# Pooled attention feeding a fast-matrix mixture of experts: ScalarE seeds the second product's bank, GpSimd keeps one sum, attention is placed a chunk ahead

## The chip, the core and the metric

The kernel runs on one core of a Trainium2 chip. Five engines work from queues of their own, each in order: TensorE (PE, with its weight loads PEld), VectorE (DVE), ScalarE (ACT), GpSimd (POOL) and SyncE (SP). They wait for each other, and for transfers, by semaphores. The metric is device time in microseconds; lower is better.

## The reference

Attention with pooled keys and values feeds a dense mixture of four experts. There are 8 batches, 8 heads, 576 tokens and a head size of 64.

```python
k_p = k.reshape(B, H, Sp, 8, D).mean(axis=3)          # 72 pooled keys
v_p = v.reshape(B, H, Sp, 8, D).mean(axis=3)
attn = softmax(q @ k_p^T / sqrt(D))
x = (attn @ v_p)  as  [B * S, H * D] = [4608, 512]
p = domain_probs / domain_probs.sum(-1)
for e in range(4):                                    # w1: 512 x 1024, w2: 1024 x 512
    out += p[:, e:e + 1] * (relu(x @ w1[e]) @ w2[e])
```

The inputs are float32; the kernel multiplies in bfloat16 and sums in float32.

## The kernel before, in words

**Chunks and tasks.** The 4608 tokens are cut into nine chunks of 512: for each batch its first 512 tokens, and a ninth chunk of the eight remainders of 64. A task is one chunk with one expert: the up product (x by w1, then ReLU, giving H) and the down product (H by w2, scaled by the token's probability and added to `acc`). Chunk 0 is done in four early stages with plain products, except for its first down product. The other 32 tasks run in one loop.

**Seven products.** In the loop each product of two matrices cut in quarters is made with seven quarter products in place of eight, from sums and differences of quarters. Of the activations these are `x_sums` (up) and `hidden_sums` (down); of the weights, `first_weight_sums` and `weight_sums`. All of them are VectorE instructions of line 186. The partial results grow in two banks of PSUM. `up_product` (L483) does this for two units of the hidden dimension, with two banks each (`units`). In step 0 ScalarE copies product 1 from bank 0 to SBUF (`partial`, L512) because it is part of several results. Step 1 makes product 2 in bank 1, and VectorE adds the copy, applies ReLU and writes a quarter of H, all in one custom instruction (`relu_sum`, L481). Steps 2 and 3 grow in bank 0 and are copied to `partial` too. Steps 4 and 6 end in `relu_sum`, step 5 in ScalarE's ReLU (L520). `down` (L550) uses the two banks `chains`; which comes first alternates from task to task. After each step two blocks of 128 tokens are added to `acc`. That is done by VectorE (`add`, L635), by ScalarE for the first write of expert 0 (L633), or, for steps in `POOLED = (1, 4, 6)` of experts 1 to 3, by ScalarE scaling into `addend` (L576) and GpSimd adding that (L578).

**Slots.** The loop counts slots `g`, seven to a task. In each slot TensorE makes step i of unit 0, step i - 1 of unit 1 (four matmuls each) and step i - 1 of the down product of the task before (eight matmuls), all with 256 columns. The order in which the program emits its instructions is by hand, and it is each engine's order. Hidden sums stand at the end of slots 0 to 3 of a task, after the reads of that slot. Pieces of attention for the next chunk are attached to slots of the 28-slot chunk (`pieces_at`).

**Attention of a batch.** GpSimd issues the loads. From batch 2 on keys and values come in four parts of two pooled rows, where parts 1 to 3 add onto the buffer during the transfer (`load_part`, L118; part 0 is L120); each therefore waits for the one before. VectorE adds the last two rows (`fold_keys`, L220; `fold_values`, L261). SP issues transposing transfers for q (`queries`, L272), keys (`keys`, L226) and, for each quarter of 128 tokens, for the context (`turn`, L339). TensorE makes `scores` (L299) and `context` (L325), ScalarE the exponential (L303), VectorE the division (L313, L314). `x_sums` needs all four turns of the batch. The remainders of two batches at a time go the same way (`rem_queries`, `rem_scores`, `rem_context`, `rem_turn`). Batch 1 is prepared in the early stages (`pieces_first`), from whole loads.

**Stores.** When expert 3 has finished a quarter of `acc`, SP stores it (L643); the next chunk's expert 0 writes that quarter again.

Of the kernel before, what the change touches and what calls it, by code (L numbers as in the profile page):

```python
# [17 lines left out]
def kernel(  # L18
# [10 lines left out]
    nc = tc.nc  # L29
# [45 lines left out]
    acc = const.tile([P, NR, DM], F32, name="acc")  # L75
    x_rem = const.tile([P, NPAIR, NT], BF16, name="x_rem")
# [174 lines left out]
    def idle(n):  # L251

        w_ps = work_bank()
        for _ in range(n):
            nc.tensor.matmul(w_ps, lhsT=zeros[:, 0:P], rhs=zeros)  # L255

# [226 lines left out]
    def up_product(c, e, unit, step):  # L483
# [5 lines left out]
            (1, False, b21, a12),  # L489
# [21 lines left out]
        if step == 0 or step == 3:  # L511
            nc.scalar.copy(out=part[:, 0], in_=ps)  # L512
        elif step == 2:
            nc.scalar.copy(out=part[:, 1], in_=ps)  # L514
        elif step == 1:
            relu_sum(quarter(0, 0), ps, part[:, 0])
        elif step == 4:
            relu_sum(quarter(1, 1), ps, part[:, 0])
        elif step == 5:
            nc.scalar.activation(out=quarter(0, 1), in_=ps, func=ACT.Relu)  # L520
        else:
            relu_sum(quarter(1, 0), ps, part[:, 1])
# [27 lines left out]
    def down(c, e, step, flip=0, pooled=()):  # L550
# [5 lines left out]
            lambda: (1, False, a12, w[:, HI, 0:HD], 0, 0, False),  # L556
# [16 lines left out]
        if step in pooled and e > 0:  # L573
            for j in range(BLOCKS):
                prob = p_all[:, c * NR + row * BLOCKS + j, e:e + 1]
                nc.scalar.activation(out=addend[:, j], in_=ps[:, j], func=ACT.Copy, scale=prob)  # L576
            dst = acc[:, row * BLOCKS:(row + 1) * BLOCKS, cols]
            nc.gpsimd.tensor_add(out=dst, in0=dst, in1=addend[:])  # L578
        else:
            for j in range(BLOCKS):  # L580
                add(ps[:, j], c, e, row * BLOCKS + j, cols, first)
# [80 lines left out]

    def pieces_first():
# [25 lines left out]
        put(3, 1, lambda: load_part(2, 1))  # L689
        put(3, 3, lambda: load_q(2))  # L690
# [4 lines left out]
    def pieces_at(b):  # L695

        at = {}

        def put(slot, piece):
            at.setdefault(slot, []).append(piece)  # L700

        if b < B:
            late = b == BUSY
            put(4 if late else 0, lambda: queries(b))
            put(5 if late else 0, lambda: fold_keys(b, every))
            put(6 if late else 1, lambda: keys(b, every))
            put(7 if late else 5, lambda: fold_values(b, every))
            for pair, slot in enumerate((9, 11, 12, 13) if late else (6, 8, 12, 13)):
                put(slot, lambda pair=pair: scores(b, pair))
            for r in range(NR):  # L710
                put((14, 16, 19, 21)[r], lambda r=r: context(b, r))
                put((15, 17, 20, 22)[r], lambda r=r: turn(b, r))
            put(26, lambda: x_sums(b))
            if late:
                put(1, lambda: load_part(b, 3))
                put(2, lambda: load_q_rem(b))
            if b + 1 < B:
                put(8 if late else 6, lambda: load_part(b + 1, 0))
                put(9 if late else 8, lambda: (load_q(b + 1), load_q_rem(b + 1)))
                put(12, lambda: load_part(b + 1, 1))  # L720
                put(17, lambda: load_part(b + 1, 2))
                put(22, lambda: load_part(b + 1, 3))
        if b % 2 == 0 and b <= B:
            i = b // 2 - 1
            put(0, lambda: rem_queries(i))
            put(4, lambda: rem_scores(i))
            put(7, lambda: rem_context(i))
            put(8, lambda: rem_turn(i))
        if b == B:
            put(12, lambda: x_sums(B))  # L730
        return at

    ENG = mybir.EngineType
    with tc.manual_schedule(
# [13 lines left out]
        load_whole(1, v, "vraw")  # L748
        load_w2(1)
        load_w1(3)  # L750
# [6 lines left out]
        first_pieces = pieces_first()  # L757

        for s, (above, below) in enumerate(
                [((0, 1), None), ((0, 2), (0, 0)), ((0, 3), (0, 1)), (None, (0, 2))]):  # L760
            if s == 1:
                hidden_sums(*below, 0)
                hidden_sums(*below, 1)
            for i in range(FCH):
                if above:
                    up(*above, (i,))
                if below and s != 1 and i % 2:
                    down_plain(*below, i // 2)
# [9 lines left out]
        units[0] = [psum_last.tile([P, NT], F32, name=f"unit0{i}") for i in range(2)]  # L778

        N = len(order)
        below_of = [(0, 3)] + order
        sums = {}
        for at, pieces in (((2, 3, 4, 5), first_weight_sums(2)), ((9, 10, 12, 13), weight_sums(2)),
                           ((16, 17, 18, 19), first_weight_sums(3))):
            sums.update(zip(at, pieces, strict=True))
        POOLED = (1, 4, 6)
        for g in range(7 * N + 1):
            t, i = divmod(g, 7)  # L790
            if t < N:
# [4 lines left out]
            if g >= 1:  # L796
                down(*below_of[t2], i2, t2 % 2, POOLED)
            if i < 4 and t < N:
                hidden_sums(*below_of[t], i)
            if t < N:  # L800
                c = order[t][0]
                at = pieces_at(c + 1)
                for piece in at.get(g - 7 * E * (c - 1), ()):
                    piece()
            if g in sums:
                sums[g]()
# [31 lines left out]
```

## Time and profile before

| | us |
|---|---|
| median of 4 runs | 515.4 (513.71 to 516.87) |
| the profiled execution | 516.33 |
| its span, first to last instruction | 514.6 |
| TensorE busy | 496.9 (97%) |
| VectorE busy | 405.6 (79%) |
| ScalarE busy | 291.9 (57%) |
| GpSimd busy | 181.9 (35%) |

The costliest groups beside TensorE are the 192 ReLU sums (131.3 us, 684 ns each), the 246 additions to `acc` of 256 columns (107.2, 477 ns), GpSimd's 72 additions (95.9, 1331 ns), ScalarE's 128 copies of line 512 (74.9, 585 ns) and its 144 scalings of line 576 (60.5, 471 ns).

A line of the timeline reads: start, length, engine, line, operation, tile written and tiles read, shape, count, and in brackets the idle time of the engine just before with what ended it. A line of the waits reads: who waited, for whom, the total in us, how often, the longest. "DMA kpT<-kp" is the transfer that writes the tile kpT from kp. A group's mean length of a matmul (273 ns for 256 columns) includes its way through the array; from start to start it is 109 ns. Idle time of an engine other than the bound costs nothing by itself.

### The profile page before, as it was taken

How to read it: one execution, taken by the hardware profiler on the slowest of the kernel's cores; microseconds unless marked ns; L12 is line 12 of the kernel's file. 1: busy time of each engine (PE TensorE's matmuls, PEld its weight loads, DVE VectorE, ACT ScalarE, POOL GpSimd, SP SyncE). 2: the span in 40 equal slices, each digit the busy share in tenths (PEclk: the TensorE clock that was granted, in tenths of full speed). 3: DMA queues.
4: the chain of work that ended last, by engine and by line, in shares of the span. 5: the costliest groups of instructions: out<-in, count | busy, mean ns of one | idle time of the engine just before them, and what ended most of it. 6: DMA issues, size and time to landing. Idle time of an engine off the chain costs nothing.

```text
span 514.6 us, 11532 instructions
## 1 busy us (share of the span) xinstructions
PE 496.9 (97%) x4578; PEld 407.6 (79%) x4578; DVE 405.6 (79%) x776; ACT 291.9 (57%) x557; POOL 181.9 (35%) x160
## 2 busy tenths in 40 slices
PE   9999897899899999999999999999999999999996
PEld 4656345678777988888878888888888888888885
DVE  3556387969997898788978896889788878877873
ACT  2675513575457656755576567655765565556550
POOL 6331053424445353535363536253102311222131
PEclk9999899989999999999999999999999999999998
DMA  9999999895819491948294849775102020003003
GB/s 190 210 206 208 186 89 88 147 87 56 75 35 153 41 100 36 150 44 95 43 143 38 94 56 114 73 88 55 64 19 35 20 75 2 0 22 83 1 1 83
DMA packets 106790, 42.51 MB, mean 83 GB/s; under 512 B 79840, under 2 KB 105184, under 8 KB 106736
## 3 DMA queue, kind: packets, MB, share of 16 engines
q0 software_dynamic: 59728, 22.43, 41.2%
q1 hardware_dynamic: 46432, 18.82, 19.1%
q8 instruction: 36, 0.59, 0.5%
q10 hardware_dynamic: 576, 0.52, 0.3%
q14 instruction: 18, 0.15, 0.1%
HBM read 45.69 MB, written 9.44 MB: 107 GB/s over the span
## 4 chain that ended last, share of the span: by engine, by line
PE 79%; DMA 10%; DVE 7%; issue 2%; ACT 1%; POOL 0%; DVEq 0%
PE unit L500 34%; PE o_ps L567 33%; DMA w_bf<-in_moe_w_dram 5%; DMA xT<-x_tok 3%; PE unit L255 2%; PE unit L448 2%; PE att L299 1%; PE unit L619 1%; PE o_ps L590 1%; DVE H L481 1%; DVE acc L635 1%; PE att L325 1%; DVE H L186 1%; DMA kpT<-kp 1%; DVE wu_bf L186 1%
## 5 line engine op out<-in xcount | busy, mean ns | idle before, releaser
L578 POOL TENSOR_TENSOR acc<-acc,addend 128x512 f32<-128x512 f32 x72 | 95.9, 1331 | 256.5 <-ACT addend L576 132.3
L481 DVE CUSTOM_DVE_ANT_0 H<-unit,partial 128x512 bf16<-128x512 f32 x192 | 131.3, 684 | 29.0 <-PE unit L500 26.3
L635 DVE SCALAR_TENSOR_TENSOR acc<-o_ps,p_all,acc 128x256 f32<-128x256 f32 (+1 forms) x254 | 113.2, 485 | 46.1 <-PE o_ps L567 34.2
L567 PEld LDWEIGHTS <-H 128*128 128x128 bf16 x1320 | 129.0, 98 | 17.1 <-DVE H L186 1.2
L500 PEld LDWEIGHTS <-w_bf 128*128 128x128 bf16 x1024 | 96.9, 98 | 17.4 <-issue 6.2
L512 ACT COPY partial<-unit 128x512 f32<-128x512 f32 x128 | 74.9, 585 | 57.2 <-PE unit L500 56.3
L567 PE MATMUL o_ps<-w_bf,H 128*128 128x256 bf16 x792 | 102.6, 273 | 0.0
L500 PE MATMUL unit<-xT,w_bf 128*128 128x256 bf16 x672 | 96.4, 273 | 1.4 <-DVE H L481 0.7
L576 ACT ACTIVATE addend<-o_ps,p_all 128x256 f32<-128x256 f32 x144 | 60.5, 471 | 53.5 <-PE o_ps L567 53.5
L500 PEld LDWEIGHTS <-wu_bf 128*128 128x128 bf16 x768 | 74.6, 98 | 12.7 <-DVE xs L186 2.4
L500 PE MATMUL unit<-xs,wu_bf 128*128 128x256 bf16 x512 | 77.6, 274 | 2.1 <-DVE xs L186 2.1
L567 PE MATMUL o_ps<-wt_bf,H 128*128 128x256 bf16 x528 | 68.5, 273 | 0.6 <-DVE H L186 0.6
L567 PEld LDWEIGHTS <-S 128*128 128x128 bf16 x528 | 51.8, 99 | 9.7 <-DVE S L186 2.9
L514 ACT COPY partial<-unit 128x512 f32<-128x512 f32 x64 | 38.0, 594 | 19.7 <-PE unit L500 18.9
L520 ACT ACTIVATE H<-unit 128x512 bf16<-128x512 f32 x64 | 38.2, 596 | 19.0 <-PE unit L500 18.9
L118 POOL DMA_DIRECT2D kraw<-in_k_dram x18 | 25.1, 1395 | 37.9 <-DMA kraw<-in_k_dram 37.9
L500 PE MATMUL unit<-xs,w_bf 128*128 128x256 bf16 x256 | 38.5, 273 | 0.0
L303 ACT ACTIVATE expT<-att 72x1024 bf16<-72x1024 f32 x28 | 28.5, 1018 | 15.8 <-PE att L299 15.8
L633 ACT ACTIVATE acc<-o_ps,p_all 128x256 f32<-128x256 f32 x72 | 30.2, 471 | 12.5 <-PE o_ps L567 10.0
L567 PE MATMUL o_ps<-wt_bf,S 128*128 128x256 bf16 x264 | 35.1, 277 | 2.1 <-DVE S L186 2.1
L118 POOL DMA_DIRECT2D vraw<-in_v_dram x18 | 33.9, 1885 | 3.6 <-DMA vraw<-in_v_dram 3.6
L567 PE MATMUL o_ps<-w_bf,S 128*128 128x256 bf16 x264 | 34.2, 273 | 0.0
(106 smaller groups left out, 486.8 us busy)
## 6 DMA issues: line engine op xcount, KB each, us to landing
out_dram<-acc SPq DMA_DIRECT2D x32, 256.0 KB, 2.5
w_bf<-in_moe_w_dram POOLq DMA_DIRECT2D x7, 1024.0 KB, 22.3
q_sb<-in_q_dram POOLq DMA_DIRECT2D x7, 512.0 KB, 9.5
kraw<-in_k_dram POOLq DMA_DIRECT2D x24, 144.0 KB, 6.2
vraw<-in_v_dram POOLq DMA_DIRECT2D x24, 144.0 KB, 8.0
acc<-in_q_dram SPq DMA_DIRECT2D x2, 512.0 KB, 4.7
w_bf<-in_moe_w_dram POOLq DMA_DIRECT2D x2, 512.0 KB, 11.6
wt_bf<-in_k_dram POOLq DMA_DIRECT2D x2, 288.0 KB, 7.6
```

The lines of the kernel that those rows point to most:

```text
L118: nc.gpsimd.dma_start(out=raw[:], in_=rows, accum_op=ALU.add)
L303: nc.scalar.activation(out=expT[:, 2 * pair:2 * pair + 2].rearrange("j h a b t -> j b (h a) t"), in_=sc_ps[0:SP].rearrange("j b h (a t) -> ...
L481: nc.vector._custom_dve(TENSOR_ADD_SAT, out=dst, in0=ps, in1=part, s0=LARGEST, s1=0.0)
L500: nc.tensor.matmul(ps[:, n * HN:(n + 1) * HN], lhsT=lhs[:, kc, f:f + P], rhs=rhs[:, kc, :], start=(not grows and n == 0 and kc == 0), stop ...
L512: nc.scalar.copy(out=part[:, 0], in_=ps)
L514: nc.scalar.copy(out=part[:, 1], in_=ps)
L520: nc.scalar.activation(out=quarter(0, 1), in_=ps, func=ACT.Relu)
L567: nc.tensor.matmul(ps[:, j], lhsT=lhs[:, i, j * P:(j + 1) * P], rhs=rhs[:, i, :], start=(not grows and i == 0 and j == 0), stop=(i == HF - 1),
L576: nc.scalar.activation(out=addend[:, j], in_=ps[:, j], func=ACT.Copy, scale=prob)
L578: nc.gpsimd.tensor_add(out=dst, in0=dst, in1=addend[:])
L633: nc.scalar.activation(out=dst, in_=o_ps, func=ACT.Copy, scale=prob)
L635: nc.vector.scalar_tensor_tensor(out=dst, in0=o_ps, scalar=prob, in1=dst, op0=ALU.mult, op1=ALU.add,)
```

## The change

- `up_product`: ScalarE copies product 1 from bank 0 into bank 1 of PSUM. Product 2 grows on top of it, and ScalarE applies ReLU to the result. Two ReLU sums per unit are left to VectorE, which add the results of steps 2 and 3.
- `down`: in the same way product 1 is copied from one bank into the other, where product 2 grows. The additions to `acc` after step 0 fall away; step 1 adds the sum. `POOLED` is `(4,)`: GpSimd does one sum per task, steps 1 and 6 go to VectorE.
- `open_bank` makes one matmul in each of two banks before they are first grown on.
- Hidden sums 0, 2 and 3 stand at the start of their slots, hidden sum 1 after unit 1's product.
- Plain products of chunk 0's experts 1 and 2 stand at other places; the last one stands in slot 0 of the loop.
- w1 of expert 3 is loaded ahead of w2 of expert 1.
- `gate`: a small GpSimd copy reads one element of each of the four turns of batch 1. It stands ahead of part 1 of batch 2 in GpSimd's queue.
- `pieces_later` gives each batch's attention its slots. For batches 4 to 7 q, keys and values are prepared in the last four slots of the chunk before, the turns are in slots 9, 10, 12 and 14, and the loads of the next batch in slots 0, 1, 4, 7 (keys and values) and 17 (q). Batches 2 and 3 have slots of their own. The fold of batch 2's keys is still in slot 5, its first scores move from 9 to 11. Weight sums move by some slots.

```diff
+    def open_bank(ps):
+        nc.tensor.matmul(ps, lhsT=ident[:], rhs=w2_bf[:, 0, 0, :], skip_group_check=True)
...
-            (1, False, b21, a12),
+            (1, True, b21, a12),
...
-        if step == 0 or step == 3:
-            nc.scalar.copy(out=part[:, 0], in_=ps)
-        elif step == 2:
-            nc.scalar.copy(out=part[:, 1], in_=ps)
+        if step == 0:
+            nc.scalar.copy(out=units[unit][1][:], in_=ps)
+        elif step == 2 or step == 3:
+            nc.scalar.copy(out=part[:, step - 2], in_=ps)
         elif step == 1:
-            relu_sum(quarter(0, 0), ps, part[:, 0])
+            nc.scalar.activation(out=quarter(0, 0), in_=ps, func=ACT.Relu)
         elif step == 4:
-            relu_sum(quarter(1, 1), ps, part[:, 0])
+            relu_sum(quarter(1, 1), ps, part[:, 1])
...
-            relu_sum(quarter(1, 0), ps, part[:, 1])
+            relu_sum(quarter(1, 0), ps, part[:, 0])
...
-            lambda: (1, False, a12, w[:, HI, 0:HD], 0, 0, False),
+            lambda: (1, True, a12, w[:, HI, 0:HD], 0, 0, True),
...
-        if step in pooled and e > 0:
+        if step == 0:
+            nc.scalar.copy(out=chains[(1 + flip) % 2][:], in_=chains[flip][:])
+        elif step in pooled and e > 0:
...
+    def gate():
+        nc.gpsimd.tensor_copy(out=gate_at[:], in_=state[("xT", 1)][0:1, 0, 0:NT:P])
...
-        put(3, 1, lambda: load_part(2, 1))
-        put(3, 3, lambda: load_q(2))
+        put(3, 1, gate, lambda: load_part(2, 1))
+        put(3, 2, lambda: load_q(2))
...
-    def pieces_at(b):
+    def pieces_later():
...
+        for b in range(2, B + 1):
+            start = 7 * E * (b - 2)
+            if b < B:
+                q_at, k_at, scores_at, contexts_at, loads_at = {
+                    2: (4, 5, (11, 12, 13, 17), (18, 19, 20, 22), (8, 10, 9, 12, 15)),
+                    3: (0, 1, (6, 11, 12, 13), (16, 18, 19, 20), (4, 6, 5, 8, 11)),
+                }.get(b, (-4, -4, (3, 4, 5, 6), (8, 9, 11, 13), (0, 17, 1, 4, 7)))
+                put(start + q_at, lambda b=b: queries(b))
+                put(start + k_at, lambda b=b: fold_keys(b, every))
+                put(start + k_at + 1, lambda b=b: keys(b, every), lambda b=b: fold_values(b, every))
...
+            if b == 2:
+                put(1, lambda: load_part(2, 3))
+                put(2, lambda: load_q_rem(2))
...
+            put(start + 26, lambda b=b: x_sums(b))
...
+        load_w1(3)
         load_w2(1)
-        load_w1(3)
...
+        plain_at = {(2, 2): 0, (2, 4): 1, (2, 6): 2, (2, 7): 3}
+        plain_at.update({(3, 2 * r + 1): r for r in range(NR - 1)})
...
+                open_bank(chains[1][:])
...
+        open_bank(units[0][1][:])
...
-        POOLED = (1, 4, 6)
+        POOLED = (4,)
         for g in range(7 * N + 1):
             t, i = divmod(g, 7)
+            if i in (0, 2, 3) and t < N:
+                hidden_sums(*below_of[t], i)
             if t < N:
                 up_product(*order[t], 0, i)
             t2, i2 = divmod(g - 1, 7)
             if 0 <= t2 < N:
                 up_product(*order[t2], 1, i2)
-            if g >= 1:
+            if i == 1 and t < N:
+                hidden_sums(*below_of[t], i)
+            if g == 0:
+                down_plain(0, 2, NR - 1)
+            else:
                 down(*below_of[t2], i2, t2 % 2, POOLED)
-            if i < 4 and t < N:
-                hidden_sums(*below_of[t], i)
```

## The prediction

> **What bounds the kernel now.** I read the page first, then TensorE's waits, then the busy time by stretches, then the timelines around each wait.
>
> ```profile
> span 514.6 us, 11532 instructions
> PE 496.9 (97%) x4578; PEld 407.6 (79%) x4578; DVE 405.6 (79%) x776; ACT 291.9 (57%) x557; POOL 181.9 (35%) x160
> ```
>
> TensorE is the bound; every other engine has room. Only its pauses can be won back, and any new pause in the loop is lost whole. Its waits, over the whole run:
>
> ```profile
> PE att L299 <- DMA kpT<-kp: 2.1, 1, 2.1
> PE o_ps L567 <- DVE S L186: 2.1, 3, 1.0
> PE unit L500 <- DVE xs L186: 2.1, 1, 2.1
> PE unit L448 <- DMA w_bf<-in_moe_w_dram: 2.0, 1, 2.0
> ...
> PE unit L500 <- DVE H L481: 0.7, 2, 0.4
> PE o_ps L567 <- DVE H L186: 0.6, 2, 0.3
> ```
>
> The stretches (us, PE busy, PEld, DVE, ACT, POOL, granted clock, DMA share, GB/s) say where:
>
> ```profile
> 53.70:60.00 6.30, 6.28 (x26) 2.14 (x27) 0.76 (x2) 2.37 (x4) 0.00 (x0) 0.73 1.29 205
> 78.00:86.00 8.00, 5.51 (x47) 4.27 (x45) 5.07 (x12) 3.01 (x7) 2.44 (x3) 1.00 1.21 70
> 97.00:101.50 4.50, 2.44 (x23) 1.93 (x20) 4.47 (x10) 1.75 (x4) 3.63 (x5) 1.00 0.85 148
> 101.50:106.30 4.80, 4.74 (x30) 3.43 (x31) 2.84 (x6) 2.92 (x5) 1.42 (x1) 0.64 1.51 138
> 422.00:492.00 70.00, 70.00 (x644) 62.74 (x642) 56.19 (x104) 41.14 (x84) 15.16 (x13) 1.00 0.08 20
> ```
>
> All pauses lie before 163 us; from there matmuls follow each other at 0.109 us per 256 columns. A slot of the loop (4 + 4 + 8 matmuls) is 1.744 us, a task of seven slots 12.2 us. After two of the three 2-us pauses the clock was halved: (1 - 0.73) x 6.3 = 1.7 us and (1 - 0.64) x 4.8 = 1.7 us lost.
>
> The Trainium skill, "TensorE: Matmul & The Clock Gate", section "What's actually happening", lets the clock fall only after about 3.4 us of idleness; here 2.0 and 2.1 us sufficed, and a third 2.1 us did nothing. By that rule (a) would win 2.0 and (b) 6.0, 3.4 us less together.
>
> **Part by part, what goes.** T is the start of the fourth early stage, 71.47 us in the trace.
>
> (a) w1 of expert 3 is loaded ahead of w2 of expert 1. In the trace w2 landed at 47.7, w1 at 53.7; TensorE stood from 51.7 to 53.7. Swapped, w1 is there by about 48.7 (a 1 MB load takes 5 to 6 us) and w2 at 53.7, needed first by VectorE's weight sums, which ran at 53.25, and by TensorE's second product four matmul groups on. Gain 2.0 plus the 1.7 of clock: -3.7, so T = 67.8.
>
> (b) The pauses in T to slot 10 of the loop. Work alone is 7.0 (four plain products, 32 x 0.216) + 0.44 + 9 x 1.744 + 0.8 (remainder scores and context) = 23.9. The trace has 101.89 - 71.47 + 1.7 of clock - 0.4 of scores = 31.7. So 7.7 us are lost there now: the xs wait 2.1, the kpT wait 2.1, the clock 1.7, the small sums the rest.
>
> (c) Pauses in 130 to 150 (S 1.0 and 0.6, H 0.45 and 0.30, latencies): 2.8. They come from a turn of batch 2 that landed after 7.2 us beside the loads, and from VectorE's lag. The loads of batch 3 now end by slot 15, the last turn is at slot 23, alone (2.4 us, as three turns of that batch), and x_sums(2) at slot 26, three slots later. The hidden sums stand a slot's work earlier in VectorE's queue. -2.8.
>
> **What the change adds.** (d) The gate. GpSimd waits until the four turns of batch 1 have landed before it issues parts 1, q, 2, 3 of batch 2.
>
> ```profile
> 65.86 1.42 POOL L118 DMA_DIRECT2D kraw<-in_k_dram  x1 [22.13 <-DMA kraw<-in_k_dram]
> 66.89 1.82 POOL L118 DMA_DIRECT2D vraw<-in_v_dram  x1
> 67.74 1.91 POOL L126 DMA_DIRECT2D q_sb<-in_q_dram  x1
> 72.84 1.40 POOL L118 DMA_DIRECT2D kraw<-in_k_dram  x1 [3.19 <-DMA kraw<-in_k_dram]
> ...
> 83.56 1.39 POOL L118 DMA_DIRECT2D kraw<-in_k_dram  x1 [6.94 <-DMA kraw<-in_k_dram]
> ```
>
> Each part adds onto the one before and is issued when that has landed: the chain ran 65.9, 72.8, 83.6 and landed at 88.75; VectorE's fold of the keys (L220) started at 93.30 without a wait. Now the fourth turn is issued at T and lands at T + 2.4 without loads beside it (10.3 with them), the gate takes 0.1 to 0.3 (the small POOL rows), so part 1 starts at T + 2.8. Keys, values, q and the next keys took 13.4 us from first issue to last landing at 153.75 to 167.18: part 2 lands at T + 16.2, part 3 is issued at T + 16.5 and lands 5.2 us later (as at 83.56) or 9.7 (as at 184.2, beside a transpose of q, which now is issued at about T + 14): T + 21.7 to T + 26.2. The fold is still at slot 5. That slot starts at T + 7.4 + 4 x 1.744 = T + 14.4, and VectorE is at the fold by T + 16.1. So it waits 5.6 to 10.1 us, with every ReLU sum behind it. The chain to TensorE: fold 0.76, ReLU sum of unit 0 step 6 0.68, ScalarE's copy 0.59, i.e. T + 23.8 to 28.3 for slot 8, due at T + 20.1. A new pause of 3.7 to 8.2 us; between the ends I take 6.0, as q's transpose overlaps the part only partly. Over 2 us long, it costs 1.7 of clock. +7.7, as much as (b) gives back: the early loop moves its wait from xs and kpT to the keys' load. Also behind the gate on POOL are q's remainder and the add of slot 5, done by about T + 22; SP's store of that quarter follows, and expert 0 rewrites it in slot 11, after T + 31: free.
>
> (e) ScalarE copies product 1 into bank 2 (up, both units; down), and product 2 then waits for that copy. The up copies have room: unit 0's step 0 is 2 x 0.436 + 0.872 ahead of step 1 less its own 0.436, 1.3 us against 0.2 + 0.59. The down copy is the tight one:
>
> ```profile
> 379.62 1.04 PE L567 MATMUL o_ps<-w_bf,H 128*128 128x256 bf16 x8
> 381.37 0.82 PE L567 MATMUL o_ps<-w_bf,H 128*128 128x256 bf16 x6
> 380.70 0.88 DVE L635 SCALAR_TENSOR_TENSOR acc<-o_ps,p_all,acc 128x256 f32<-128x256 f32 x2 [0.15 <-PE o_ps L567]
> 379.82 0.59 ACT L512 COPY partial<-unit 128x512 f32<-128x512 f32 x1 [0.25 <-PE unit L500]
> ```
>
> Product 1's readers can start at 380.70, product 2 starts at 381.37: 0.67 us for a copy of 0.59 and a hand-over of 0.05. ScalarE is free: its copy for unit 1 ends at 380.47. Nothing in the trace writes PSUM from ScalarE; the nearest row is the same 128x512 copy to SBUF, 0.585 to 0.594, which I take; the ends are 0.47 (L576, half as wide) and 1.02 (L303, twice as wide). At 0.59 the pause is 0, at 1.02 it is 0.4 x 32 tasks = 13 us. For stray lateness (an expT of 1.02, POOL's port holding an S sum for 1.4 instead of 0.68) I put 0.03 x 32 = +1.0.
>
> The Trainium skill, "PSUM — Partial Sum Buffer", section "Specifications (TRN2)", calls ScalarE's writes to PSUM faster than to SBUF; no row shows it, and it would leave the pause at 0. That page's section "Summary: rules for kernel authors" speaks against the step: only zero may be seeded from ScalarE, other seeds go through TensorE. That would be a product's worth of extra matmuls (0.3 to 0.9 us each) and more than the gain; here two matmuls at the start prepare the banks instead.
>
> (f) Engine loads. ReLU sums 192 to 128 (-64 x 0.684 on DVE, +64 x 0.596 on ACT); pooled evictions 144 to 48 (-96 x 0.471 on ACT), POOL adds 72 to 24 (-48 x 1.331); DVE adds +30 x 0.477; 33 down copies on ACT, +19. DVE -29 us, ACT +12, POOL -64. None is on the path after 163 us: 0.
>
> (g) Attention of batches 4 to 7 a chunk ahead: turns were in time already (no wait after 163): 0. But keys' parts are issued in slots 0, 1, 4, 7. With 5.2 to 6.7 us per landing, part 2 leaves POOL at 15 us into the chunk, and the add of slot 5 and its store, then the store of slot 6 on SP behind it, come 5 us later than now: landing at 19.3 to 22, and expert 0 rewrites that quarter at 21.4. I take 0; at the late end 2.5 us in each of three chunks.
>
> (h) The two bank-opening matmuls, 0.2 each; the plain products' places; weight sums moved within slots: 0, under TensorE's own work.
>
> Sum: -3.7 - 7.7 - 2.8 + 7.7 + 1.0 = -5.5. The profiled execution took 516.33 (span 514.6 and 1.7 around it): 510.8 there. The median of four is 515.4, 0.9 lower: **510 us**.
>
> **Rivals.** *The loads come in time* (q's transpose and q hardly slow the parts): the new pause shrinks to about 1 without clock loss, -12.2: 503. For it: turns no longer compete; against: 13.4 us for the same sequence of loads undisturbed. *The down copy holds TensorE*: 0.67 us is the whole allowance. Slower than before from (5.5 / 32) + 0.62 = 0.8 us per copy on, measurably from 0.88; at 1.02, 515.4 - 5.5 + 13 = 523. For it: no margin, 32 times; against: the 0.59 row. *Stores late behind the part loads* (g): 3 x 2.5 = 7.5, 517.4, no change that a measurement can tell; for it: POOL and SP work in order; against: loads of 5 to 6 us when nothing else runs.
>
> **Numbers.** Forecast 0.55, loads in time 0.13, down copy 0.20, late stores 0.12. A measurement tells 0.5% (2.6 us) from no change: faster is under 512.8, slower over 518.0. The forecast's own range is 506 to 514 (pause 3.7 to 8.2, clock or not, strays 0 to 3). Faster: 0.85 of the forecast and all of the first rival, 0.60; slower: most of the down copy and a little of the late stores, 0.21; same: 0.19. Range 502 to 521, from the first rival's end to near the second's.
>
> **What would show it.** Right: no wait of L448 on w_bf; DVE's L220 with some 5 to 10 us before it at about 84, and TensorE's longest pause right behind, at 88 to 95, with a halved clock; none for xs, kpT or S. L500 and L567 waiting on ScalarE's copy after 163 would mean (e) is wrong; ScalarE's L633 waiting on out's store, (g). I would be wrong above all if the copy into PSUM takes over 0.65 us, or the fold doesn't wait.

## The result and the profile after

The changed kernel took 515.9 us in the median (512.67 to 523.63, 53 runs) against 514.35 for the kernel before (79 runs): a ratio of 1.0037, with a 95% interval of 1.0024 to 1.005. That is 1.9 us slower, where 510 was forecast. The ratio compares the means of the fast runs (49 of the changed kernel's 54, those up to 520.3 us), so it is not the quotient of the two medians. The time lies inside the stated range and the change inside the half per cent called "same", but the interval lies wholly above 1, on the wrong side.

The head of the page and the rows of the two groups that matter most below, of the changed kernel:

```profile
span 514.4 us, 11277 instructions
PE 496.9 (97%) x4580; PEld 408.3 (79%) x4580; DVE 375.0 (73%) x742; ACT 301.8 (59%) x558; POOL 119.9 (23%) x113
...
L505 PE MATMUL unit<-xT,w_bf 128*128 128x256 bf16 x672 | 97.6, 275 | 9.9 <-ACT unit L518 9.9
...
L518 ACT COPY unit<-unit 128x512 f32<-128x512 f32 x64 | 37.1, 580 | 39.6 <-PE unit L505 22.3
```

VectorE fell by 31 us, GpSimd by 62, ScalarE rose by 10: the forecast's -29, -64 and +12. TensorE is as busy as before, and its matmuls of line 505 now wait 9.9 us for ScalarE's new copy (L518), which the page before could not have. TensorE's waits from 50 to 165 us, and then from 165 to 500 us, where the kernel before had none:

```profile
PE unit L505 <- ACT unit L518: 4.5, 1, 4.5
PE att L304 <- DMA kpT<-kp: 0.2, 1, 0.2
...
PE unit L505 <- ACT unit L518: 5.4, 7, 0.9
```

The waits for w1, the xs sums, the keys, the hidden sums and the ReLU sums, 9.6 us in all, are gone but for 0.2. One wait of 4.5 us has come in the early loop and seven of under 1 us later. The stretches of the changed kernel (columns as before: us, PE, PEld, DVE, ACT, POOL, granted clock, DMA share, GB/s):

```profile
53.70:60.00 6.30, 6.30 (x41) 2.66 (x40) 3.45 (x6) 4.49 (x8) 0.00 (x0) 1.00 1.28 206
78.00:86.00 8.00, 8.00 (x87) 6.99 (x86) 7.10 (x14) 4.88 (x10) 2.89 (x3) 1.00 1.39 142
88.00:101.50 13.50, 9.00 (x69) 6.56 (x67) 7.64 (x16) 5.21 (x10) 7.48 (x8) 0.75 1.32 146
101.50:106.30 4.80, 4.80 (x46) 3.59 (x45) 3.09 (x6) 3.96 (x9) 3.31 (x4) 1.00 1.00 84
163.00:377.00 214.00, 208.61 (x2050) 179.20 (x2049) 166.78 (x330) 135.10 (x249) 52.56 (x44) 1.00 0.60 74
422.00:492.00 70.00, 70.00 (x667) 62.37 (x665) 51.02 (x100) 42.64 (x84) 6.02 (x5) 1.00 0.09 22
```

and the one stretch that was not shown of the kernel before:

```profile
163.00:377.00 214.00, 213.50 (x2090) 184.06 (x2088) 179.87 (x350) 134.37 (x256) 86.94 (x70) 1.00 0.65 76
```

At 54, 78 and 102 us the holes are filled and the clock is whole. There is a new hole between 88 and 101.5 us, with the clock at 0.75. From 163 to 377 us TensorE is busy 208.6 of 214 us, and was 213.5: the loss lies where no change was forecast.

To add this up I took, for each matmul, the distance from its start to the next one's start, less the usual distance for the same line and tiles (the median). The sum over a stretch, called the excess below, is the time that TensorE took above its work, halved clock included:

| stretch, us | before | after | measured | forecast |
|---|---|---|---|---|
| 51 to 80 | 4.39 | 0.89 | -3.5 | (a) -3.7 |
| 80 to 130 | 9.06 | 8.77 | -0.3 | (b) -7.7, (d) +7.7 |
| 130 to 165 | 3.98 | 1.11 | -2.9 | (c) -2.8 |
| 165 to 500 | 6.17 | 12.13 | +6.0 | (e) +1.0 |

The profiled executions took 516.33 before and 516.46 after. They are 2.0 and 0.6 above the medians of their kernels, so the table's sum of -0.7 and the measured +1.9 do not contradict each other; the split is what the table is good for.

**Two kinds of pause after 165 us.** All seven stand ahead of step 1 of a unit. TensorE waits for ScalarE's copy into that unit's second bank; the copy must wait until VectorE's last ReLU sum (L486) of the task before has read that bank; and VectorE is late. The first kind came at 188, 242, 296 and 351 us, at 0.93 us of lost time each. The timeline of the changed kernel at 240 us:

```profile
239.78 0.42 DVE L187 TENSOR_TENSOR xs<-xs,xT 128x512 bf16<-128x512 bf16 x1
240.08 1.27 POOL L587 TENSOR_TENSOR acc<-acc,addend 128x512 f32<-128x512 f32 x1 [11.02 <-ACT addend L585]
240.12 1.51 DVE L187 TENSOR_TENSOR xT<-xT 128x512 bf16<-128x512 bf16 x1
241.56 0.41 DVE L187 TENSOR_TENSOR xs<-xT,xs 128x512 bf16<-128x512 bf16 x1
241.89 0.68 DVE L486 CUSTOM_DVE_ANT_0 H<-unit,partial 128x512 bf16<-128x512 f32 x1
242.66 0.57 ACT L518 COPY unit<-unit 128x512 f32<-128x512 f32 x1 [2.14 <-DVE H L486]
243.28 1.03 PE L505 MATMUL unit<-xT,w_bf 128*128 128x256 bf16 x8 [0.77 <-ACT unit L518]
```

The sums of the activations now follow the folds of keys and values of slots 24 and 25, and meet GpSimd's one addition of the task. A sum that takes 0.42 us takes 1.51 when GpSimd's addition starts 0.04 us ahead of it. So it is at all four places, and in the traces of e1, e2, e4 and e7 as well, with a pause of 0.93 us each. At 401 us no batch is left to fold, and the addition starts only when this sum is done:

```profile
401.22 0.42 DVE L187 TENSOR_TENSOR xT<-xT 128x512 bf16<-128x512 bf16 x1
401.62 1.48 POOL L587 TENSOR_TENSOR acc<-acc,addend 128x512 f32<-128x512 f32 x1 [11.02 <-ACT addend L585]
```

There the same sum takes 0.42 us, so does the next one (it started 0.07 us ahead of the addition), and TensorE makes no pause. The second kind came at 218, 273 and 327 us (0.64, 1.09 and 1.07 us lost). The timeline at 271 us:

```profile
271.32 0.69 DVE L319 TENSOR_TENSOR x_tok<-att,inv 128x512 bf16<-128x512 f32 x1 [1.49 <-DMA xT<-x_tok]
271.93 0.68 DVE L187 TENSOR_TENSOR S<-H 128x1024 bf16<-128x1024 bf16 x1
272.53 0.68 DVE L486 CUSTOM_DVE_ANT_0 H<-unit,partial 128x512 bf16<-128x512 f32 x1
273.30 0.57 ACT L518 COPY unit<-unit 128x512 f32<-128x512 f32 x1 [1.12 <-DVE H L486]
273.92 0.60 PE L505 MATMUL unit<-xT,w_bf 128*128 128x256 bf16 x4 [0.93 <-ACT unit L518]
```

VectorE's division for the fourth quarter waits 1.49 us: there are three buffers of `x_tok`, and the first quarter's turn has not left its buffer. That turn was issued at 260.67 and took 10.56 us, beside the next batch's load of q, issued at 260.59 and landed at 273.2. The load is written for slot 17 of the chunk, but nothing stood ahead of it in GpSimd's queue, so it was issued some seven slots early, on top of the turns. Between the division and the ReLU sum stands, besides, a hidden sum of 0.68 us, which the change moved to the start of its slot; no run here takes that one away.

### The profile page after: what moved, and what is told of

It is laid out like the page before. It is cut to its first block, busy times and chain, and to the rows that moved or that the text cites. A ratio compares the mean times of both kernels' runs of the same rounds, so it can differ in the third digit from the quotient of the medians.

```text
span 514.4 us, 11277 instructions
## 1 busy us (share of the span) xinstructions
PE 496.9 (97%) x4580; PEld 408.3 (79%) x4580; DVE 375.0 (73%) x742; ACT 301.8 (59%) x558; POOL 119.9 (23%) x113
## 4 chain that ended last, share of the span: by engine, by line
PE 77%; DMA 13%; DVE 7%; issue 2%; ACT 1%; DVEq 0%; ACTq 0%; POOLq 0%; SPq 0%; POOL 0%
PE o_ps L573 32%; PE unit L505 31%; DMA xT<-x_tok 8%; PE unit L453 4%; DMA kraw<-in_k_dram 4%; PE unit L256 2%; PE att L304 2%; DVE H L486 2%; PE unit L628 1%; DMA kpT<-kp 1%; DVE xT L187 1%; ACT unit L518 1%; DVE xs L187 1%; PE att L330 1%; DVE x_tok L319 1%
## 5 line engine op out<-in xcount | busy, mean ns | idle before, releaser
L644 DVE SCALAR_TENSOR_TENSOR acc<-o_ps,p_all,acc 128x256 f32<-128x256 f32 (+1 forms) x284 | 126.3, 485 | 56.3 <-PE o_ps L573 38.2
L505 PEld LDWEIGHTS <-w_bf 128*128 128x128 bf16 x1024 | 98.3, 98 | 26.1 <-issue 14.0
L486 DVE CUSTOM_DVE_ANT_0 H<-unit,partial 128x512 bf16<-128x512 f32 x128 | 87.6, 685 | 25.8 <-PE unit L505 19.7
L573 PE MATMUL o_ps<-w_bf,H 128*128 128x256 bf16 x792 | 103.8, 275 | 0.0
L587 POOL TENSOR_TENSOR acc<-acc,addend 128x512 f32<-128x512 f32 x24 | 33.0, 1376 | 269.9 <-ACT addend L585 269.9
L520 ACT COPY partial<-unit 128x512 f32<-128x512 f32 x128 | 72.0, 589 | 33.7 <-PE unit L505 32.8
L518 ACT COPY unit<-unit 128x512 f32<-128x512 f32 x64 | 37.1, 580 | 39.6 <-PE unit L505 22.3
L522 ACT ACTIVATE H<-unit 128x512 bf16<-128x512 f32 x64 | 38.7, 605 | 26.4 <-PE unit L505 26.4
L526 ACT ACTIVATE H<-unit 128x512 bf16<-128x512 f32 x64 | 38.1, 596 | 25.8 <-PE unit L505 25.6
L642 ACT ACTIVATE acc<-o_ps,p_all 128x256 f32<-128x256 f32 x72 | 30.3, 471 | 12.2 <-PE o_ps L573 11.7
L119 POOL DMA_DIRECT2D kraw<-in_k_dram x18 | 26.3, 1461 | 36.8 <-DMA kraw<-in_k_dram 36.6
L505 PE MATMUL unit<-xT,wu_bf 128*128 128x256 bf16 x224 | 33.7, 273 | 0.0
## 6 DMA issues: line engine op xcount, KB each, us to landing
q_sb<-in_q_dram POOLq DMA_DIRECT2D x7, 512.0 KB, 11.4
```

Of the source, the lines that this page charges most:

```text
L119: nc.gpsimd.dma_start(out=raw[:], in_=rows, accum_op=ALU.add)
L486: nc.vector._custom_dve(TENSOR_ADD_SAT, out=dst, in0=ps, in1=part, s0=LARGEST, s1=0.0)
L505: nc.tensor.matmul(ps[:, n * HN:(n + 1) * HN], lhsT=lhs[:, kc, f:f + P], rhs=rhs[:, kc, :], start=(not grows and n == 0 and kc == 0), stop ...
L518: nc.scalar.copy(out=units[unit][1][:], in_=ps)
L520: nc.scalar.copy(out=part[:, step - 2], in_=ps)
L522: nc.scalar.activation(out=quarter(0, 0), in_=ps, func=ACT.Relu)
```

## The experiments

All ratios are to the kernel before, with 95% intervals; microseconds in brackets are against the changed kernel's 1.0037, worked out with 514.35 us to the whole.

### e1_xtok4: a fourth buffer for the turns

```diff
-    name="x_tok", bufs=3
+    name="x_tok", bufs=4
...
```

> A fourth x_tok buffer for the context, nothing else. In the changed kernel VectorE's division waits 1.0 to 1.5 us in three chunks for the first turn to leave its buffer (4.8 us in all), and TensorE pauses at 218, 273 and 327 us for 0.64, 1.09 and 1.07 us. Theory 'slow turns hold the buffer': those three pauses go, -2.8 us, and the other four of 0.93 us, after the x sums, stay; ratio to before about 0.998 where the changed kernel had 1.0037. Rival 'the seeding copy is late wherever VectorE is late': the division no longer waits but the sums behind it come late all the same, and half or more of the three pauses stays.

Measured: 514.14 us, ratio 1.0013 [0.9996, 1.0031] (-1.2). TensorE's waits from 165 to 500 us:

```profile
PE unit L505 <- ACT unit L518: 3.1, 4, 0.8
```

The three pauses of the second kind, 2.8 us in the profiled execution of the changed kernel, are not there; the four others are, at 0.93 us lost each as before. But the three are not there in the profiled executions of e3, e4 and e7 either, which leave both the buffers and q's load as they were: in these three VectorE waits for the buffer 0.2 us in all after 165 us, and TensorE doesn't stop for it. So this run does not show that the fourth buffer took the pauses away, and its gain is not clear of noise (the intervals of the two ratios overlap).

### e2_qgate: q's load behind the turns

```diff
-    def gate():
-        nc.gpsimd.tensor_copy(out=gate_at[:], in_=state[("xT", 1)][0:1, 0, 0:NT:P])
+    def gate(b=1):
+        nc.gpsimd.tensor_copy(out=gate_at[:], in_=state[("xT", b)][0:1, 0, 0:NT:P])
...
+                if b >= 4:
+                    put(start + q_too, lambda b=b: gate(b))
                 put(start + q_too, lambda b=b: load_q(b + 1), lambda b=b: load_q_rem(b + 1))
```

> GpSimd waits for the four turns of the batch before it issues the next q (batches 4 to 6), by the same small copy as the gate of batch 1; three x_tok buffers as before. Theory: q, written down for slot 17 but issued at slot 9 because nothing stands before it in GpSimd's queue, is what slows the turns from 2.4 to 10 us. Then the turns land in 2.4 to 5 us, the division doesn't wait, and the three pauses go as with the fourth buffer, -2.8 us. Rival 'part 3 of the keys and values slows them': the turns still take 7 us or more and the pauses stay. If q then lands too late for its transpose, a new wait of kpT or qT would show at the start of the next chunk.

Measured: 514.66 us, ratio 1.0015 [0.9997, 1.0034] (-1.1). q's loads were issued at 220.47, 274.22 and 326.98, behind the turns, and the first turns took 6.8 to 8.5 us in place of 10.1 to 10.6. The same four pauses stay, and the other three are not there, but as with e1 that shows little. In e3, e4 and e7, with q's load on top of them, the first turns took 7.4 to 9.2 us. So a first turn without q's load is nearly as slow as these, and the 2.4 to 5 us that were expected did not come; the second turns show the load, with 5.9 to 6.7 us in place of 9.1 to 11.8. The chain from the slow turn over the held buffer to TensorE stands in the changed kernel's trace, at 271 us; what makes it long enough to stop TensorE in that execution and not in others stays open.

### e3_xsums: the sums of the activations ahead of the crowd

```diff
-            put(start + 26, lambda b=b: x_sums(b))
+            put(start + {2: 26, 3: 23, B: 26}.get(b, 22), lambda b=b: x_sums(b))
```

> The x sums of batches 4 to 7 move from slot 26 to slot 22, of batch 3 to slot 23; nothing else. In the changed kernel one of the four sums takes 1.51 us instead of 0.42 in the chunks that pause, while GpSimd's addition of slot 26 runs. Theory 'GpSimd's addition holds VectorE up just ahead of the ReLU sum that the seeding copy waits for': the four pauses of 0.93 us after 165 us go, -3.5 us. Rival 'too much work for VectorE in slots 24 to 26': the sums in slot 22 make other pauses and less than half is won.

Measured: 511.94 us, ratio 0.9979 [0.9948, 1.0009] (-3.0). TensorE's waits from 165 to 500 us:

```profile
PE unit L505 <- ACT unit L518: 0.9, 2, 0.7
PE o_ps L573 <- ACT o_ps L581: 0.4, 2, 0.2
```

The four pauses of the first kind are gone (4 x 0.93 = 3.7 was the price). One of 0.7 us at 447 us is new, in a chunk without attention: there a sum of the remainders takes 1.49 us beside GpSimd's addition. What this edit can't separate is GpSimd's hold of the sum from the mere amount of VectorE's work in slots 24 to 26; the rows at 240 and 401 us do that, and e10 below.

### e4_fold: batch 2's keys folded three slots later

```diff
-                    2: (4, 5, (11, 12, 13, 17), (18, 19, 20, 22), (8, 10, 9, 12, 15)),
+                    2: (4, 8, (13, 16, 17, 18), (19, 20, 22, 23), (9, 11, 10, 12, 15)),
```

> Batch 2 alone: the fold of its keys moves from slot 5 to 8, its keys' transpose and the fold of the values to 9, scores to 13, 16, 17, 18, contexts to 19, 20, 22, 23, part 0 of batch 3's load to 9 and q to 11. Theory 'VectorE waits in its queue for the keys' part 3': the pause of 4.5 us at 88 us and the 3.4 us of halved clock behind it go, -6 to -8 us, less about 1 where the fold still waits. Rival 'the wait only moves to the scores or to the x sums of batch 2': TensorE pauses there instead by 2 us or more, and less than 4 us is won.

Measured: 511.34 us, ratio 0.9954 [0.9925, 0.9983] (-4.3, less than the 6 to 8 expected). TensorE's waits from 50 to 165 us:

```profile
PE att L304 <- DMA kpT<-kp: 2.6, 2, 1.5
PE o_ps L573 <- ACT acc L642: 0.5, 1, 0.5
PE att L330 <- DVE x_tok L319: 0.2, 1, 0.2
```

The pause of 4.5 us and the halved clock behind it are gone (the granted clock of 88 to 101.5 us is 1.00). A new wait for the transposed keys of 1.1 us at 101 us takes part of it back: the keys' turn is issued three slots later too. (The other, of 1.5 us at 142 us, is for batch 3's keys; e2, e7 and e10 have it as well, at 1.6 to 1.7 us, without this edit.) So the excess of 80 to 130 us fell from 8.77 to 3.63, not to nothing.

### e5_all4: these four edits together

```diff
-    name="x_tok", bufs=3
+    name="x_tok", bufs=4
...
-                    2: (4, 5, (11, 12, 13, 17), (18, 19, 20, 22), (8, 10, 9, 12, 15)),
+                    2: (4, 8, (13, 16, 17, 18), (19, 20, 22, 23), (9, 11, 10, 12, 15)),
...
+                if b >= 4:
+                    put(start + q_too, lambda b=b: gate(b))
...
-            put(start + 26, lambda b=b: x_sums(b))
+            put(start + {2: 26, 3: 23, B: 26}.get(b, 22), lambda b=b: x_sums(b))
```

> The four edits together on the changed kernel: fourth x_tok buffer, q behind the turns, x sums in slot 22, batch 2's fold in slot 8. If the four mechanisms are separate and are all that the change lost, the pauses after 80 us shrink to 2 or 3 us from about 14: -10 to -13 us against the changed kernel, ratio to before 0.980 to 0.985. If pauses only move when one is taken away, less than 6 us is won.

Measured: 506.48 us, ratio 0.9852 [0.9815, 0.9888] (-9.5). The single gains sum to 1.2 or 1.1 (both edits aim at one pause), 3.0 and 4.3, that is 8.5; together they are worth that and 1 us more, within the intervals, and a little less than the 10 expected. The pauses did not merely move when others were taken away. The timeline of e5_all4 at the largest pause left:

```profile
116.17 1.38 POOL L119 DMA_DIRECT2D vraw<-in_v_dram  x1 [0.52 <-DMA vraw<-in_v_dram]
116.45 2.95 DVE L187 TENSOR_TENSOR S<-H 128x1024 bf16<-128x1024 bf16 x1
117.01 1.84 POOL L587 TENSOR_TENSOR acc<-acc,addend 128x512 f32<-128x512 f32 x1
...
120.72 0.60 PE L505 MATMUL unit<-xT,w_bf 128*128 128x256 bf16 x4 [1.48 <-ACT unit L518]
```

It is the first kind again, now with a hidden sum: 2.95 us in place of 0.68, beside GpSimd's issue of a load and its addition.

### e6_swap: in the kernel before, only w1 of expert 3 ahead of w2 of expert 1

```diff
+        load_w1(3)
         load_w2(1)
-        load_w1(3)
         load_w2(2)
```

> The kernel before with only w1 of expert 3 loaded ahead of w2 of expert 1. The prediction's step (a): the pause of 2.0 us at 52 us goes, and with it the halved clock (1.7), -3.7 us. If the halved clock does not come in every execution, the median gains 2.0 to 3. Rival: the early loop absorbs it, as its waits are set by transfers: less than 1 us.

Measured: 511.77 us, ratio 0.9953 [0.9926, 0.998], 2.4 us faster than the kernel before. Step (a) put it at 3.7, of which 1.7 was the clock. The windows of e6_swap:

```profile
53.70:60.00 6.30, 6.29 (x40) 2.66 (x40) 2.77 (x5) 3.56 (x6) 0.00 (x0) 1.00 1.30 204
88.00:101.50 13.50, 10.85 (x98) 8.52 (x96) 11.58 (x22) 6.34 (x12) 7.36 (x7) 0.87 1.13 165
```

The pause at 52 us is gone. One halving remained in the early loop here, behind the 2.4 us wait for the keys.

### e7_nogate: the changed kernel without the gate

```diff
-        put(3, 1, gate, lambda: load_part(2, 1))
+        put(3, 1, lambda: load_part(2, 1))
```

> The changed kernel without the gate ahead of batch 2's part 1, all else as changed. The prediction's step (d): the loads start some 5 us sooner, the turns land later (8 to 10 us) and x_sums(1) waits about 2 to 3 us; the fold of the keys waits less, 0 to 3 us instead of 5.3. If the gate costs what (d) says, TensorE's pause at 88 us shrinks to under 2 us while one of about 2 us comes back at 78 to 80: -2 to -4 us. If the gate pays, +1 or more.

Measured: 514.37 us, ratio 1.0000 [0.9969, 1.0031] (-1.9, an interval that overlaps that of the changed kernel, so unclear). A pause of under 2 us was expected; it is longer than with the gate. VectorE's wait for the keys in e7_nogate, and then TensorE's longest:

```profile
DVE kp L221 <- DMA kraw<-in_k_dram: 6.9, 1, 6.9
...
PE unit L505 <- ACT unit L518: 6.1, 1, 6.1
```

Without the gate part 1 is under way before the turns are done (67.14 to 73.44), but then part 2 takes 74.03 to 82.05 and part 3 82.33 to 92.27, 9.94 us beside q's transpose (80.65 to 92.44). With the gate the three parts took 4.95, 7.62 and 5.63 us, and the last landed at 91.11. The fold waits 6.9 us in place of 5.3. So the gate is not what makes the fold late; a fold in slot 5 is late with or without it.

### e8_seed: in the kernel before, only the seeding

```diff
...
-            (1, False, b21, a12),
+            (1, True, b21, a12),
...
+        if step == 0:
+            nc.scalar.copy(out=units[unit][1][:], in_=ps)
...
+        if step == 0:
+            nc.scalar.copy(out=chains[(1 + flip) % 2][:], in_=chains[flip][:])
...
-        POOLED = (1, 4, 6)
+        POOLED = (4,)
```

> The kernel before with only the seeding copies, the ReLU by ScalarE, POOLED = (4,) and the two bank-opening matmuls; loads, attention slots and hidden sums as before. The prediction's step (e): the copies alone cost 0 to 1 us, so the time is that of before within 0.3%. Rival 'seeding puts ScalarE and VectorE on TensorE's path': pauses before step 1 of the up and down products in every chunk, with about 1 us at each place where VectorE is late (context, x sums): +5 us or more over 32 tasks.

Measured: 510.44 us, ratio 0.9937 [0.9909, 0.9964], 3.2 us faster than the kernel before, where the steps (e) and (f) had +1 and 0. After 165 us the excess is 5.81 (6.17 before): TensorE waits for a copy once, 0.2 us, in the old order. From 130 to 165 us it fell from 3.98 to 0.86, and from 80 to 130 from 9.06 to 7.69.

### e9_seedswap: seeding and swap

```diff
-        load_w2(1)
         load_w1(3)
+        load_w2(1)
...
-            (1, False, b21, a12),
+            (1, True, b21, a12),
...
-        POOLED = (1, 4, 6)
+        POOLED = (4,)
```

> The kernel before with two parts of the change, the seeding (with POOLED = (4,)) and the swap of the two weight loads; attention slots, hidden sums, gate as before. The seeding alone measured 0.9937, the swap alone 0.9953. If they are separate: 0.989, 5.5 us faster than before, so that what the whole change loses against this (1.0037) is made by the moved slots, the gate and the order of the loads: 7 us. If the two win the same pauses in the early loop: 0.992 to 0.994.

Measured: 508.84 us, ratio 0.9893 [0.9858, 0.9927]. The two gains add up to 5.5 us. The changed kernel holds both and stands at 1.0037, so all the rest of the change (slots, gate, order of the other loads, places of hidden sums and plain products) costs 1.0037 - 0.9893 = 1.44%, 7.4 us. In the early loop the trace has the changed kernel's new pause in small, without a gate: the fold of batch 2's keys waits 3.4 us, and TensorE 3.2 us for the copy behind it.

### e10_slots4: the changed kernel with batches 4 to 7 in their old slots

```diff
-                }.get(b, (-4, -4, (3, 4, 5, 6), (8, 9, 11, 13), (0, 17, 1, 4, 7)))
+                }.get(b, (0, 0, (6, 8, 12, 13), (14, 16, 19, 21), (6, 8, 12, 17, 22)))
...
-                put(start + k_at + 1, lambda b=b: keys(b, every), lambda b=b: fold_values(b, every))
+                put(start + k_at + 1, lambda b=b: keys(b, every))
+                put(start + (k_at + 1 if b < 4 else 5), lambda b=b: fold_values(b, every))
...
-                put(start if b == 2 else start - 3, lambda i=i: rem_queries(i))
-                put(start + (5 if b == 2 else 16), lambda i=i: rem_scores(i))
+                put(start, lambda i=i: rem_queries(i))
+                put(start + (5 if b == 2 else 4), lambda i=i: rem_scores(i))
...
```

> The changed kernel with the slots of the kernel before for batches 4 to 8 (queries and fold in slot 0, scores 6 to 13, contexts 14 to 21, loads 6, 8, 12, 17, 22); batches 2 and 3, the gate and all else as changed. Theory 'the chunk-ahead slots bring the waits after 165 us': no wait of the division for a turn's buffer, and the x sums of batches 4 to 7 no longer stand behind a fold in slots 24 and 25; they still meet GpSimd's addition in slot 26, so one to three pauses of 0.9 us may stay. -2 to -5 us against the changed kernel, ratio 0.994 to 1.000. Rival: seeding needs the chunk-ahead slots, and the folds in slots 0 to 5 make the copies late: +2 us or more.

Measured: 510.84 us, ratio 0.9928 [0.9902, 0.9954] (-5.6). TensorE's waits from 165 to 500 us:

```profile
PE unit L505 <- ACT unit L518: 0.7, 1, 0.7
```

Only the pause at 447 us is left, and the excess of the stretch is 6.00, as before the change. The early pause (5.4 us in this execution) is still there. The sums of the activations still stand in slot 26, but no folds stand ahead of them, and in none of the four chunks is one held:

```profile
238.58 0.42 DVE L187 TENSOR_TENSOR xs<-xT,xs 128x512 bf16<-128x512 bf16 x1
238.65 1.48 POOL L587 TENSOR_TENSOR acc<-acc,addend 128x512 f32<-128x512 f32 x1 [8.81 <-ACT addend L585]
```

So of the 7.4 us, 5.6 go to the attention placed a chunk ahead, the remainders' pieces and the loads of the next batch with it. The other 1.8, no more than the intervals leave open, are what the early loop's rearrangement comes to.

### e11_best2: e5 with batch 2's scores later still

```diff
-                    2: (4, 8, (13, 16, 17, 18), (19, 20, 22, 23), (9, 11, 10, 12, 15)),
-                    3: (0, 1, (6, 11, 12, 13), (16, 18, 19, 20), (4, 6, 5, 8, 11)),
+                    2: (4, 8, (16, 17, 18, 19), (20, 21, 22, 23), (9, 11, 10, 12, 15)),
+                    3: (0, 1, (9, 11, 12, 13), (16, 18, 19, 20), (4, 6, 5, 8, 11)),
```

> The kernel with the four edits, and in it the scores of batch 2 in slots 16 to 19, its contexts in 20 to 23, and batch 3's first scores in slot 9 instead of 6. The two pauses of 1.1 us for kpT at 99 and 142 us go, -2 us: ratio 0.981 where the four edits had 0.985. If the later contexts make x_sums(2) wait for the turns, a pause of 1 us or more comes back at 130 us and the time stays.

Measured: 504.70 us, ratio 0.9817 [0.9783, 0.9851], 9.4 us faster than the kernel before. The head of its page:

```profile
span 503.4 us, 11282 instructions
PE 492.3 (98%) x4580; PEld 406.6 (81%) x4580; DVE 376.4 (75%) x742; ACT 300.7 (60%) x558; POOL 119.8 (24%) x116
```

The keys' waits of e4 are gone and the excess of 80 to 130 us is 3.18.

### e12_all4_nogate: e5 without the gate of batch 1

```diff
-        put(3, 1, gate, lambda: load_part(2, 1))
+        put(3, 1, lambda: load_part(2, 1))
```

> The kernel with the four edits, without the gate of batch 1. The fold of batch 2's keys stands in slot 8, so the later loads no longer hold VectorE. If the gate pays by the turns alone: x_sums(1) waits for turns of 8 to 10 us, TensorE pauses 1 to 2 us at about 78 us, ratio 0.988 to 0.990 where the gated one had 0.985. If the gate is worth nothing with TensorE's early pause gone: 0.985 within the interval.

Measured: 504.43 us, ratio 0.9813 [0.9772, 0.9853], not slower than e5 as the gate's worth would have it. TensorE's waits from 50 to 165 us, all of them:

```profile
PE att L304 <- DMA kpT<-kp: 0.3, 1, 0.3
```

With the fold three slots later nothing in this early loop needs the gate. Whether leaving it out gains anything is open, since the intervals of e5 and e12 overlap. e11 and e12 are the fastest versions found; both beat the kernel before and the changed one.

## Why the prediction was wrong, by its steps

**(a), the swap: right.** -3.5 in the table against -3.7, and T came out at 68.31 against 67.8. Alone (e6) it is worth 2.4 us, with an interval from 1.0 to 3.8. The profiled execution before had the clock halved behind that pause, and the forecast counted those 1.7 us as if every run paid them; in e8 a wait of 1.6 us at the same place had no halving.

**(b) and (d), the early loop: right in sum and size, wrong in cause.** The two were to cancel, and the stretch moved by -0.3. e12, which has neither the old waits nor the new one, leaves 1.59 there: (b) is worth 9.06 - 1.59 = 7.5 (forecast 7.7), and (d) 8.77 - 1.59 = 7.2 (forecast 7.7). The timeline of the changed kernel shows (d) link by link as forecast:

```profile
91.13 0.76 DVE L221 TENSOR_TENSOR kp<-kraw 72x512 bf16<-72x512 bf16 x2 [5.33 <-DMA kraw<-in_k_dram]
91.81 0.68 DVE L486 CUSTOM_DVE_ANT_0 H<-unit,partial 128x512 bf16<-128x512 f32 x1
92.58 0.57 ACT L518 COPY unit<-unit 128x512 f32<-128x512 f32 x1 [5.55 <-DVE H L486]
93.20 1.86 PE L505 MATMUL unit<-xT,w_bf 128*128 128x256 bf16 x8 [4.50 <-ACT unit L518]
```

The fold waits 5.33 us (5.6 to 10.1 forecast) and TensorE 4.50 (3.7 to 8.2, 6.0 taken). The clock was at half for 6.8 us, 5.8 of them with TensorE at work again, so it cost 2.9 us where 1.7 was put. But the forecast hung the wait on the gate, and e7 and e9 have it without the gate. What takes it away is a later fold (e4). The keys' last part lands no sooner without the gate (92.27 in e7, 91.11 with it): part 1 leaves 4.9 us earlier, but each part takes longer beside the turns, q's load and q's transpose.

**(c): about right in size, on the wrong ground.** -2.9 against -2.8, which was put down to new slots for turns and sums; in e1, e2 and e10, which leave the slots of that stretch as the change has them, it is -1.5 to -2.1. e8 moves no slot and gets 3.98 - 0.86 = 3.1. The forecast read a slow turn of batch 2 and VectorE's lag as the ground. The turn held VectorE for 0.25 us. The lag has a ground that the forecast did not read, in the trace before:

```profile
138.15 1.27 POOL L578 TENSOR_TENSOR acc<-acc,addend 128x512 f32<-128x512 f32 x1 [4.54 <-ACT addend L576]
138.23 1.47 DVE L186 TENSOR_TENSOR xs<-xs,xT 128x512 bf16<-128x512 bf16 x1
141.02 1.03 PE L500 MATMUL unit<-xT,w_bf 128*128 128x256 bf16 x8 [0.45 <-DVE H L481]
...
145.74 2.06 POOL L578 TENSOR_TENSOR acc<-acc,addend 128x512 f32<-128x512 f32 x1 [2.82 <-ACT addend L576]
146.64 1.70 DVE L186 TENSOR_TENSOR H<-H 128x1024 bf16<-128x1024 bf16 x1
148.40 0.83 PE L567 MATMUL o_ps<-wt_bf,H 128*128 128x256 bf16 x6 [0.30 <-DVE H L186]
```

GpSimd's additions lengthen VectorE's sums here too, by 1.05 and 1.02 us ahead of the waits of 0.45 and 0.30, and by 0.73 and 0.52 some instructions ahead of those of 1.01 and 0.63. In e8, where GpSimd has 24 additions in place of 72, no such sum of the whole run takes over 0.70 us. So the fewer additions of `POOLED = (4,)` are the likely ground; VectorE's lighter queue, 31 us less over the run, is the rival, and no run separates the two.

**(e), the copies: right for the down copy, wrong for the up copies.** The tight one held: the copy into PSUM takes 0.570 us in the median (0.59 to SBUF was taken), the down product's bank leaves 0.67, and TensorE paused for it in none of the 32 tasks of the profiled execution. The up copies, to which the forecast gave room of 1.3 us, are the ones that TensorE waits for: 5.4 us after 163 us, the forecast's own sign that (e) is wrong. The room was worked out from TensorE's end alone: from product 1 to step 1. The copy has a second condition, that the bank it writes to has been read by the last ReLU sum of the task before, and the forecast didn't count that. After 163 us ScalarE's copy waits for that sum seven times, 11.4 us in all.

**(f), engine loads at 0: a gain missed.** Together with (e) the seeding is worth -3.2 us (e8); the waits for VectorE's sums at 130 to 150 us are the part that the traces show. Since (c) had booked most of that gain on another ground, the total is not wrong by it, which is luck.

**(g), attention a chunk ahead at 0: the step that failed.** It cost 5.6 us (e10 against the changed kernel; 6.0 in the table against 1.0 for strays). The forecast asked whether turns land in time, and they do. It looked at the stores as the late case, and ScalarE's L642 never waits for one after 163 us. What it didn't ask is what else stands in VectorE's queue in the slots given: the folds of slots 24 and 25 push the sums of slot 26 onto GpSimd's addition, which is worth 3.0 us (e3; e10 has the same sums in the same slot without the folds, and none is held). The table's +6.0 holds both kinds of pause; in the traces of e4 and e7, which have the first kind alone, the stretch has 9.2 us, 3.0 above before. The other 2.6 us are not divided: each part is known to 1 or 2 us either way, and the held buffer, with 1.2 and 1.1 us in e1 and e2, is not clear of noise. And it takes the seeding to pass VectorE's lateness on: in the kernel before no ScalarE copy of 0.57 us and hand-over lies between the ReLU sum and TensorE's step 1. e8 and e10 show that the copies without these slots are harmless; the slots without the copies were not tried.

**(h)** at 0: nothing in the traces speaks against it.

**The rivals.** *Loads in time* fell with the fold's wait of 5.33 us, *the down copy* with 0.570 us, *late stores* with no wait for a store. The rival that came true, an up copy held by a late VectorE, was not among them.

**Open.** What makes the second kind of pause and which executions get it, and so how much of the changed kernel's wide spread of 512.67 to 523.63 is due to it; whether the hidden sums at the start of their slots take part in it. What the gate is worth anywhere.

## What to carry to other kernels

A step handed from a busy engine to an idle one still has to wait for the busy engine's reads: work out its room from every condition on the tile that it writes, not from the one that the change is about. A slot in an emission order is an order, not a time: a transfer with nothing ahead of it in its queue leaves when it can (here q's load, some seven slots early), onto whatever is in flight then. And when pieces are moved, list for each slot they go to what the engine that feeds the critical one has there already, and what GpSimd does at that moment.

## What the runs showed of the hardware

**A sum beside GpSimd.** VectorE's sum of two bf16 tiles in SBUF took 1.51 us in place of 0.42 beside a GpSimd addition of 1.27 us that had started 0.04 us earlier, and 2.95 in place of 0.68 beside a GpSimd load issue and an addition. The slower sum of 512 columns ends 0.28 us after GpSimd's addition, as if it had waited for it. In the traces of both kernels and the twelve runs all 24 sums of this size that began during an addition (0.04 to 0.28 us after its start) took 1.47 to 1.51 us, and all 126 that had begun before one (by 0.02 us or more) took 0.42 or 0.43. The Trainium skill, "SBUF — State Buffer", section "Who interferes with whom", says that an instruction with two SBUF inputs contends with a GpSimd instruction that reads SBUF; the 1.51 against 0.42 us agrees. One stray of this kind was in the forecast (1.4 in place of 0.68), though not that it would fall on the same place in four chunks.

**The clock.** It was halved for 3.4 us behind pauses of 2.0 and 2.1 us (before), 2.4 (e6) and 3.7 (e8), and for 6.8 us behind 4.5 (after); after 5.4 us (e10) it was 3.4. A third pause of 2.1 us (before) and one of 3.2 us (e9) had no halving. Here a pause of two to three microseconds cost its length, and 1.7 us more in some executions.

**Copies within PSUM.** ScalarE's 128x512 float32 copy from bank to bank took 0.570 us in the median and the same one to SBUF 0.587.
